# Constant products in front of the transposes and the value products of a fused attention and MoE kernel

## The chip, the cores and the metric

One NeuronCore of one Trainium2 chip. The metric is device time in microseconds, the median of several runs of one launch.

## The reference

Attention with 4 batches, 8 heads, head size 64, 512 local tokens with a window of 32 to either side, and 32 global tokens that attend to all and are attended to by all; then a dense feed-forward layer (512 to 2048 to 512), then a layer of 8 experts that picks one for each of 2176 tokens.

```
s_ll = where(|i - j| <= 32, q_l k_l^T / 8, -1e9);  s_lg = q_l k_g^T / 8
out_l = softmax([s_lg, s_ll]) [v_g, v_l];  out_g = softmax(q_g [k_g, k_l]^T / 8) [v_g, v_l]
x = [out_g, out_l], heads side by side
h = x w_in;  x = max(0.01 h, h) w_out
e = argmax(norm(x) norm(emb)^T / tau);  y = p_e * (relu(x w1[e]) w2[e])
```

## The kernel before

Heads go in twos: 16 head pairs `n`, and each has two score pairs `p` of two 128-row chunks. For one `p`, `S` (L186) adds the mask as a product of `identb` and `mask` into a PSUM bank and the scores on top of it, VectorE takes the maximum (`nm`), ScalarE the exponentials (`pr`), VectorE divides. `TR` (L235) transposes the probabilities of one unit (`p` has two units `u`) into the bank `pp`, four transposes, and ScalarE copies them to `pT`. `AV` (L244) multiplies them with the values into the bank `av`, 16 products, and ScalarE or VectorE copies the result to `xr`. `QK` (L157) transposes queries and keys; `GS`, `GT` and `GA` do the same for the global tokens of two head pairs (`sg`, `gp`, `ga`).

`att_parts` (L975) lays these parts into 68 slots, one unit each: `S` in the even slots, `TR` two units and `AV` four units behind. Slots 0 to 20 run alone (`while slot < SLOT0`). In that time the banks come from the table `ALONE`; `pp` has the two buffers of tag `Y` for itself, `av` shares tag `T`. From slot 21 on the remaining slots are dealt out among the steps of the feed-forward layer (`L1` gives `hps` and `gf`, `L2` gives `yp`), and `bank` is another table.

The feed-forward weights come as 8-byte numbers and are converted on the chip, 32 pieces: `conv_load` fetches `raw` (512 KB, two buffers), `conv_round` makes `t` from it (ScalarE, two instructions), `conv_bits` joins the halves (VectorE, three instructions), `conv_split` casts to the high part (ScalarE) and subtracts for the low part (GpSimd). `conv()` stands in most slots of the alone part and in each of the first feed-forward steps, and the pieces must be done before the steps that use them.

TensorE runs in the order in which the code is written (`manual_schedule`). At this place of the program the other engines and the SP queue are ordered by a scheduler, by priorities and a timeline of its own.

Of the kernel before, what the change touches and what calls it, by code (L numbers as in the profile page):

```python
# [24 lines left out]
def kernel(  # L25
# [16 lines left out]
    nc = tc.nc  # L42
# [5 lines left out]
    E, _, F2 = w1.shape  # L48
# [6 lines left out]
    WK = WIN + SG  # L55
# [48 lines left out]
    def load_v(n):  # L104
# [21 lines left out]
    mask = att.tile([P, 3, WK], BF16, name="mask")  # L126
    nc.vector.memset(mask, 0.0)
    nc.gpsimd.affine_select(
        out=mask[:, :, 0:WIN], in_=mask[:, :, 0:WIN], pattern=[[0, 3], [1, WIN]],
# [3 lines left out]
        out=mask[:, :, 0:WIN], in_=mask[:, :, 0:WIN], pattern=[[0, 3], [-1, WIN]],  # L133
# [6 lines left out]
    identb = att.tile([P, P], BF16, name="identb")  # L140
# [8 lines left out]
    ALONE = dict(sp0="S", sp1="H", sg1="S", pp="Y", av="T", gp="Y", gq="T", ga="T", qp="T", kp="H", gnp="S")  # L149
    bank = ALONE  # L150

    def bank_of(name):
        return bank[name] if name in bank else "T"
# [32 lines left out]
    def S(p):  # L186
# [45 lines left out]
        for h in range(2):  # L232
            units[2 * p + h] = pr2[h]

    def TR(u):  # L235
        pr = units[u]
        pp = ps.tile([P, 4, P], F32, tag=bank_of("pp"), name="pp")
        for j in range(4):
            nc.tensor.transpose(pp[:, j, :], pr[:, j // 2, (j % 2) * P:(j % 2) * P + P], ident)  # L239
        pT = att.tile([P, 4, P], F32, tag="PT", bufs=2, name="pT")  # L240
        nc.scalar.copy(pT, pp)
        units[u] = pT

    def AV(p):  # L244
        n, c0 = p // 2, 2 * (p % 2)
        b, hp = n // HP, n % HP
        pTs = [units.pop(2 * p + h) for h in range(2)]
        ve, vb = values[n]
        av = ps.tile([P, 2, P], F32, tag=bank_of("av"), name="av")
        for i in range(2):  # L250
            for j, v in enumerate((ve, vb)):
                for h in range(2):
                    nc.tensor.matmul(  # L253
                        av[D * h:D * h + D, i, :], v[:, c0 + i, h, :], pTs[h][:, 2 * i + j, :],
                        start=(j == 0), stop=(j == 1), tile_position=(0, D * h),
                    )
        k = 2 * b + p % 2
        if hp == 0:
            xraw[k] = sb.tile([P, KM, 256], F32, tag="xr", bufs=4, name="xr")
        if hp == HP - 1:  # L260
            rows_done.add(k)
        (nc.vector.tensor_copy if p % 2 else nc.scalar.copy)(xraw[k][:, hp, :].rearrange("k (c s) -> k c s", c=2), av)
# [712 lines left out]
    def att_parts(n):  # L975

        parts = []
        m = n // 4
        if m % 2 == 1 and n % 4 == 0 and m < NHP:
            parts.append(lambda: GS(m))  # L980
        if n < NU and n % 2 == 0:
            parts.append(lambda: ahead(50, S, n // 2))
        if 1 == 1 and n % 4 == 3 and m + 1 < NHP:
            parts.append(lambda: ahead(50, QK, m + 1, 1))
        if (n - AVL) % 2 == 0 and 0 <= n - AVL < NU:
            parts.append(lambda: ahead(0, AV, (n - AVL) // 2))
        if m % 2 == 1 and n % 4 == 3 and m < NHP:
            parts.append(lambda: GA(m))
        if 0 <= n - LAG < NU:
            parts.append(lambda: ahead(50, TR, n - LAG))  # L990
        if m % 2 == 1 and n % 4 == 2 and m < NHP:
            parts.append(lambda: GT(m))
        for v in range(2, NHP):
            if n == 4 * (v - 2) + max(AVL + 2, 7 - v % 2):
                parts.append(lambda v=v: load_v(v))
        if n in (AVL + 12, AVL + 14):
            parts.append(lambda: split_x((n - AVL - 12) // 2))
        if n % 4 == 1 and m + 1 < NHP:
            parts.append(lambda: ahead(50, QK, m + 1, 0))
        if 1 == 0 and n % 4 == 3 and m + 1 < NHP:  # L1000
            parts.append(lambda: ahead(50, QK, m + 1, 1))
        return parts
# [57 lines left out]
    while k < len(steps):  # L1060
# [18 lines left out]
        bank = FUSED if (i, f) < (2, 1) else MIXED  # L1079
# [11 lines left out]
        n = (len(halves) + 1) // 2  # L1091
# [136 lines left out]
```

## Time and profile before

| | |
|---|---|
| time, median of 3 runs | 917.76 us (916.94 to 918.02) |
| profiled execution | 921.5 us, span 919.7 us |
| mean granted TensorE clock | 0.965 of full |
| TensorE busy | 869.8 us (95%), 5600 products |
| VectorE, ScalarE, GpSimd busy | 623.5, 566.3, 191.1 us |
| moved by DMA | 92.67 MB |

Busy time is the time in which an engine had an instruction under way. The ends of TensorE's products are modelled, so neighbours overlap in their lengths, and the distance between starts is the better price of one. A granted clock of 1.00 is 2.4 GHz, of 0.50 it is 1.2 GHz.

### The profile page before, as it was taken

The numbers are of one execution on the slowest core, as the hardware profiler recorded it, in microseconds if no ns is written. First come the engines' busy times: TensorE is split into PE (matmuls) and PEld (weight loads), VectorE is DVE, ScalarE is ACT, GpSimd is POOL, SyncE is SP. The second block draws the span as 40 slices with busy tenths as digits, with TensorE's granted clock in tenths as the row PEclk, the third lists the DMA queues.
The fourth block names the chain that finished last, engine by engine and source line by source line (L and its number), as shares of the span: only waits on it lengthen the run. The fifth ranks groups of instructions, "written<-read, shape, count | busy, mean of one in ns | idle before, by whom it ended". The sixth has DMA issues, their size and how long they took to land.

```text
span 919.7 us, 15811 instructions
## 1 busy us (share of the span) xinstructions
PE 869.8 (95%) x5600; PEld 726.0 (79%) x5600; DVE 623.5 (68%) x1419; ACT 566.3 (62%) x1243; POOL 191.1 (21%) x220
## 2 busy tenths in 40 slices
PE   6778789999999999999999999997999999999997
PEld 3546577888888888888888889886787888888885
DVE  6788788444563645463543425557998999999996
ACT  6887776544544645444533223347887888888885
POOL 3433434000200110010000000020366322231211
PEclk7787799999999999999999999999999999999999
DMA  8786463120122021110000000560316119729550
GB/s 233 188 207 176 127 169 93 27 53 12 32 63 45 20 58 34 33 36 9 1 24 1 24 1 22 190 225 12 47 36 229 58 46 338 282 85 383 184 203 26
DMA packets 104994, 92.67 MB, mean 101 GB/s; under 512 B 73735, under 2 KB 82055, under 8 KB 104914
## 3 DMA queue, kind: packets, MB, share of 16 engines
q1 hardware_dynamic: 98290, 78.52, 27.7%
q0 software_dynamic: 4224, 10.78, 4.1%
q10 hardware_dynamic: 2400, 2.36, 0.9%
q8 instruction: 45, 0.74, 0.4%
q14 instruction: 35, 0.29, 0.1%
HBM read 140.03 MB, written 11.63 MB: 165 GB/s over the span
## 4 chain that ended last, share of the span: by engine, by line
PE 72%; DMA 8%; issue 6%; DVE 5%; ACT 5%; POOL 2%; SPq 0%; POOLq 0%; ACTq 0%; DVEq 0%
PE hps L680 21%; PE hp L910 8%; PE yp L702 7%; PE yp L938 7%; PE yp L704 7%; PE yp L703 6%; PE av L253 3%; PE pp L239 3%; PE sp L202 2%; DMA out_dram<-yo,ids 2%; POOL xg L854 2%; DMA ids<-idl 1%; ACT pr L223 1%; PE ga L314 1%; PE lp L504 1%
## 5 line engine op out<-in xcount | busy, mean ns | idle before, releaser
L687 ACT COPY gf<-hps 128x256 f32<-128x256 f32 (+1 forms) x144 | 50.2, 360 | 179.4 <-PE hps L680 178.6
L688 DVE SCALAR_TENSOR_TENSOR gf<-gf 128x256 f32<-128x256 f32 (+1 forms) x144 | 59.7, 422 | 137.2 <-ACT gf L687 136.7
L910 PE MATMUL hp<-w1s,xgT 128*128 128x512 f32 x528 | 137.7, 409 | 3.1 <-DVE xgT L899 3.1
L938 PE MATMUL yp<-w2s,ht 128*128 128x512 f32 x528 | 131.0, 396 | 1.0 <-DVEq L1192 1.0
L938 PEld LDWEIGHTS yp<-w2s,ht 128*128 128x128 f32 x528 | 98.8, 188 | 25.6 <-DVEq L1192 1.4
L910 PEld LDWEIGHTS hp<-w1s,xgT 128*128 128x128 f32 x528 | 98.1, 193 | 24.9 <-DVE xgT L899 4.4
L702 PE MATMUL yp<-woh,g 128*128 128x512 f32 x272 | 115.2, 424 | 0.2 <-ACT g L690 0.2
L704 PE MATMUL yp<-woh,g 128*128 128x512 f32 x272 | 108.0, 397 | 1.1 <-DVE g L691 1.1
L703 PE MATMUL yp<-wol,g 128*128 128x512 f32 x272 | 107.9, 397 | 0.0
L691 DVE TENSOR_TENSOR g<-gf,g 128x256 fp32r<-128x256 f32 (+1 forms) x144 | 60.7, 431 | 42.9 <-ACT g L690 39.9
L680 PE MATMUL hps<-xs,wih 128*128 128x256 f32 x448 | 75.8, 291 | 2.7 <-ACT gf L687 2.7
L690 ACT CAST g<-gf 128x256 fp32r<-128x256 f32 (+1 forms) x144 | 55.4, 395 | 34.2 <-DVE gf L688 34.0
L680 PEld LDWEIGHTS hps<-xs,wih 128*128 128x128 f32 x448 | 65.1, 190 | 9.2 <-ACT gf L687 3.1
L680 PE MATMUL hps<-xs,wil 128*128 128x256 f32 x448 | 71.7, 282 | 0.0
L680 PE MATMUL hps<-xl,wih 128*128 128x256 f32 x448 | 71.7, 282 | 0.0
L946 POOL DMA_INDIRECT out_dram<-yo,ids x22 | 33.8, 1537 | 143.6 <-ACT yo L945 129.7
L704 PEld LDWEIGHTS yp<-woh,g 128*128 128x128 f32 x272 | 51.4, 189 | 14.5 <-DVE g L691 2.1
L680 PEld LDWEIGHTS hps<-xs,wil 128*128 128x128 f32 x448 | 61.4, 190 | 0.0
L680 PEld LDWEIGHTS hps<-xl,wih 128*128 128x128 f32 x448 | 61.4, 190 | 0.0
L702 PEld LDWEIGHTS yp<-woh,g 128*128 128x128 f32 x272 | 51.5, 189 | 12.0 <-issue 4.3
L854 POOL DMA_INDIRECT xg<-x2d,ids x24 | 48.2, 2010 | 60.9 <-PE hps L680 21.6
L865 DVE TENSOR_TENSOR w2s<-w2a,w2s 128x1024 fp32r<-128x1024 f32 x48 | 56.4, 1216 | 3.1 <-ACT w2s L864 3.1
(261 smaller groups left out, 1751.5 us busy)
## 6 DMA issues: line engine op xcount, KB each, us to landing
w1a<-in_moe_w_dram SPq DMA_DIRECT2D x12, 2048.0 KB
w2a<-in_moe_w_dram SPq DMA_DIRECT2D x12, 2048.0 KB
w1b<-in_moe_w_dram SPq DMA_DIRECT2D x12, 2048.0 KB
w2b<-in_moe_w_dram SPq DMA_DIRECT2D x12, 2048.0 KB
raw<-in_moe_w_in_dram SPq DMA_DIRECT2D x14, 512.0 KB
raw<-in_moe_w_out_dram SPq DMA_DIRECT2D x14, 512.0 KB
x2d<-x SPq DMA_DIRECT2D x16, 256.5 KB
kn<-in_k_l_dram SPq DMA_DIRECT2D x31, 128.0 KB
```

The costliest lines, as they stand in the source:

```text
L680: nc.tensor.matmul(hps, ws[a][:, k], xs[c][k], start=(a + c + k == 0), stop=((a, c) == (1, 0) and k == KM - 1))
L687: nc.scalar.copy(gf, hps[:, cs])
L688: nc.vector.scalar_tensor_tensor(out=gf, in0=gf, scalar=0.01, in1=gf, op0=ALU.mult, op1=ALU.max)
L690: nc.scalar.copy(g[:, 0], gf)
L691: nc.vector.tensor_tensor(out=g[:, 1], in0=gf, in1=g[:, 0].bitcast(F32), op=ALU.subtract)
L702: nc.tensor.matmul(yp, g[:, 0], hi, start=(f == 0), stop=False)
L703: nc.tensor.matmul(yp, g[:, 0], lo, start=False, stop=False)
L704: nc.tensor.matmul(yp, g[:, 1], hi, start=False, stop=(f == KF - 1))
L854: nc.gpsimd.indirect_dma_start(out=xg, out_offset=None, in_=x2d[:, :], in_offset=bass.IndirectOffsetOnAxis(ap=ids[:, s:s + 1].bitcast(U32) ...
L865: nc.vector.tensor_tensor(out=w[:, 1, c], in0=src[:, c], in1=w[:, 0, c].bitcast(F32), op=ALU.subtract)
L910: nc.tensor.matmul(hp_, xT[:, a, k, :], w[:, c, k, :], start=(a + c + k == 0), stop=(c == 1 and k == KM - 1))
L938: nc.tensor.matmul(yp, ht[:, a, f, :], w[:, c, f, :], start=(j + a + c + f == 0), stop=(j == c == 1 and f == 3))
```

## The change

While `bank` is `ALONE` (slots 0 to 20), `TR` and `AV` first issue products of `identb` and `mask` into the bank that they have just been given, with start and stop set, so that the products proper overwrite them: 5 ahead of the transposes of an even unit, 2 ahead of those of an odd one (448 columns each), and 8 ahead of the value products (256 columns each).

```diff
+    def spin(out, n):
+
+        if bank is not ALONE:
+            return
+        o = out.rearrange("p a b -> p (a b)")
+        m = min(o.shape[1], 2 * WK)
+        for _ in range(n):
+            nc.tensor.matmul(
+                o[:, 0:m], identb, mask.rearrange("p a b -> p (a b)")[:, 0:m], start=True, stop=True
+            )
+
     def TR(u):
         pr = units[u]
         pp = ps.tile([P, 4, P], F32, tag=bank_of("pp"), name="pp")
+        spin(pp, 5 if u % 2 == 0 else 2)
         for j in range(4):
...
         av = ps.tile([P, 2, P], F32, tag=bank_of("av"), name="av")
+        spin(av, 8)
         for i in range(2):
```

TensorE, the transposes of the two units of the second score pair, and the keys of the next head pair behind them, before:

```order
L253 MATMUL av<-pT,vb_104 64x128 x2
L239 MATMUL pp<-ident,pr_98 128x128 x8
L174 MATMUL kp<-ident,kn 128x128 x4
L179 MATMUL gnp<-ident,gn 128x64
L197 LDWEIGHTS identb
```

And with the change, from the first of the two units on:

```order
L251 MATMUL pp<-ident,pr_98 128x128 x4
L242 LDWEIGHTS identb
L242 MATMUL pp<-mask,identb 128x448
L242 LDWEIGHTS identb
L242 MATMUL pp<-mask,identb 128x448
L251 MATMUL pp<-ident,pr_98 128x128 x4
L174 MATMUL kp<-ident,kn 128x128 x4
```

The eight transposes that stood together have two products between them; five more stand ahead of the first four, and eight of 256 columns ahead of the value products. Over the program there are 68 and 72 of them. The order of TensorE's other instructions is unchanged.

VectorE, from the division of the eighth score pair to the maximum of the ninth (`t` is a weight conversion, three rows each; `nm` the maximum), before:

```order
L229 TENSOR_TENSOR pr_98<-pr_98,sm 128x4x224
L370 SCALAR_TENSOR_TENSOR t_1164<-t_1163,t_1164 128x512
L373 TENSOR_SCALAR t_1163<-t_1163 128x512
L318 COPY xgl<-ga 128x2x32
L374 ISA t_1163<-t_1163,t_1164 128x1024
L370 SCALAR_TENSOR_TENSOR t_1201<-t_1200,t_1201 128x512
L212 TENSOR_REDUCE nm<-sp 128x2 x2
```

And with the change:

```order
L229 TENSOR_TENSOR pr_98<-pr_98,sm 128x4x224
L383 SCALAR_TENSOR_TENSOR t_1341<-t_1340,t_1341 128x512
L386 TENSOR_SCALAR t_1340<-t_1340 128x512
L387 ISA t_1340<-t_1340,t_1341 128x1024
L383 SCALAR_TENSOR_TENSOR t_1395<-t_1394,t_1395 128x512
L331 COPY xgl<-ga 128x2x32
L386 TENSOR_SCALAR t_1394<-t_1394 128x512
L387 ISA t_1394<-t_1394,t_1395 128x1024
L383 SCALAR_TENSOR_TENSOR t_1461<-t_1460,t_1461 128x512
L386 TENSOR_SCALAR t_1460<-t_1460 128x512
L387 ISA t_1460<-t_1460,t_1461 128x1024
L212 TENSOR_REDUCE nm<-sp 128x2 x2
```

Three conversions stand where one and the start of a second stood, and a fourth follows between this maximum and the division.

VectorE at the last of the 32 conversions (`gf` is a feed-forward step), before:

```order
L370 SCALAR_TENSOR_TENSOR t_2113<-t_2112,t_2113 128x512
L227 TENSOR_SCALAR sm<-sm 128x4
L373 TENSOR_SCALAR t_2112<-t_2112 128x512
L228 RECIPROCAL sm<-sm 128x4
L374 ISA t_2112<-t_2112,t_2113 128x1024
L688 SCALAR_TENSOR_TENSOR gf<-gf 128x256
```

And with the change:

```order
L383 SCALAR_TENSOR_TENSOR t_2253<-t_2252,t_2253 128x512
L704 TENSOR_TENSOR g<-gf,g 128x256
L386 TENSOR_SCALAR t_2252<-t_2252 128x512
L701 SCALAR_TENSOR_TENSOR gf<-gf 128x256
L387 ISA t_2252<-t_2252,t_2253 128x1024
L217 ISA pr_97,nm<-sp,mask 128x224
```

The `gf` behind the last conversion is the tenth of VectorE before; with the change the `gf` ahead of its last row is the sixth. On ScalarE, 20 conversions were finished ahead of the first `gf`, and 24 are now.

## Rows read from the trace of the kernel before

**Rows 1.** The page's 40 slices of the span: the granted TensorE clock in tenths.

```profile
PEclk7787799999999999999999999999999999999999
```

**Rows 2.** Busy time by program stage: us, then engines with instructions, clock, DMA share, GB/s.

```profile
12.70:97.00 84.30, 66.97 (x506) 45.68 (x505) 69.03 (x137) 68.45 (x191) 33.43 (x38) 0.76 0.73 192
97.00:112.00 15.00, 8.82 (x38) 7.28 (x38) 13.00 (x24) 11.80 (x33) 6.54 (x6) 0.66 0.52 149
112.00:157.00 45.00, 40.81 (x315) 34.16 (x314) 39.81 (x86) 34.26 (x85) 19.16 (x15) 0.96 0.49 134
157.00:300.00 143.00, 142.99 (x1123) 123.33 (x1122) 70.17 (x260) 68.71 (x209) 11.65 (x23) 1.00 0.16 37
```

The five busy columns are TensorE's products, its weight loads, VectorE, ScalarE and GpSimd.

**Rows 3.** The same view, stretches at the lower clock; the last lies in 112 to 157 us.

```profile
12.70:22.90 10.20, 8.06 (x40) 4.38 (x38) 8.68 (x17) 8.66 (x26) 4.36 (x5) 0.50 0.88 229
...
29.70:36.60 6.90, 5.84 (x31) 4.18 (x31) 5.77 (x15) 5.65 (x15) 4.14 (x8) 0.51 0.85 224
...
40.00:46.80 6.80, 6.80 (x54) 5.01 (x52) 2.88 (x6) 3.95 (x8) 2.56 (x2) 0.50 0.76 225
...
57.10:60.50 3.40, 3.16 (x18) 1.26 (x20) 3.40 (x10) 3.40 (x12) 0.12 (x1) 0.51 0.66 148
...
67.30:74.10 6.80, 6.28 (x34) 4.46 (x33) 6.09 (x11) 5.12 (x16) 1.33 (x2) 0.50 0.58 177
...
77.50:84.40 6.90, 6.90 (x63) 5.25 (x61) 5.65 (x8) 3.79 (x9) 2.73 (x2) 0.51 0.64 168
...
139.00:142.40 3.40, 3.40 (x16) 2.95 (x16) 3.17 (x6) 3.14 (x7) 1.64 (x1) 0.50 0.20 55
```

**Rows 4.** TensorE's waits, 12 to 97 us: us in total, times, longest.

```profile
PE sp L197 <- ACT pr L223: 6.9, 4, 2.7
PE ga L314 <- ACT gt L299: 3.1, 2, 1.6
PE sg L274 <- DVE xr L262: 2.2, 1, 2.2
PE av L253 <- ACT pT L241: 2.1, 4, 0.8
PE pp L239 <- DVE pr L229: 2.0, 2, 1.4
PE qp L162 <- DVE xr L262: 1.6, 2, 0.9
```

**Rows 5.** TensorE's timeline at 67 us: start, us, instruction, idle before it.

```profile
67.82 0.53 PE L197 MATMUL sp<-mask,identb 128*128 128x448 bf16 x1 [2.74 <-ACT pr L223]
```

**Rows 6.** The chain that ended last, 77 to 86 us: start, us, what.

```profile
77.21 2.54 PE ga L314 x40
...
80.80 0.75 PE sp L197 x2
...
84.87 1.02 PE pp L239 x8
```

**Rows 7.** TensorE's timeline, products of 256 columns at the two clock levels.

```profile
106.48 1.05 PE L680 MATMUL hps<-xl,wih 128*128 128x256 f32 x4
107.33 1.06 PE L680 MATMUL hps<-xs,wil 128*128 128x256 f32 x4
...
127.14 0.63 PE L680 MATMUL hps<-xl,wih 128*128 128x256 f32 x4
127.61 0.63 PE L680 MATMUL hps<-xs,wil 128*128 128x256 f32 x4
```

**Rows 8.** Groups of VectorE's instructions, 12.7 to 97 us: busy, mean ns, idle before.

```profile
L370 DVE SCALAR_TENSOR_TENSOR t<-t,t 128x512 int32<-128x512 int32 x17 | 13.6, 805 | 5.6 <-ACT t L363 4.1 <-ACT t L364 1.6
L374 DVE CUSTOM_DVE_ANT_0 t<-t,t 128x1024 uint16<-128x1024 uint16 x17 | 11.5, 684 | 0.1
...
L373 DVE TENSOR_SCALAR t<-t 128x512 int32<-128x512 int32 x17 | 9.5, 570 | 0.6
```

**Rows 9.** TensorE's waits, 97 to 160 us.

```profile
PE pp L239 <- ACT gf L687: 2.8, 1, 2.8
```

## The prediction

> **What bounds the kernel now.** I read the page in slices first, for the clock; then the table of busy times over stretches that I cut by program stage and by clock; then TensorE's waits and the chain of waits; last the rows that give a price.
>
> The slices show TensorE's granted clock at full for the whole run but for the first eighth [rows 1]. The stage table says what that eighth is [rows 2]. From 12.7 to 97 us the attention runs alone: TensorE is busy 66.97 of 84.3 us at a mean clock of 0.76, VectorE 69.03 and ScalarE 68.45, so three engines are near 80% and none is full. From 97 to 112 and from 112 to 157 us the first feed-forward steps run, while the conversion of their weights still goes on; there TensorE is busy 8.82 of 15 and 40.81 of 45 us. From 157 us it is busy 142.99 of 143 us. So whatever brings TensorE earlier to its place of 157 us moves the end by as much, and nothing behind it changes.
>
> The stretches at the lower of the two clock levels (1.2 GHz, shown as 0.50 or 0.51) lie in rows 3. Six are in the alone stage, 41.0 us long, with 8.06 + 5.84 + 6.80 + 3.16 + 6.28 + 6.90 = 37.0 us of busy TensorE; at 2.4 GHz half of that, 18.5 us, would not be there. TensorE's 84.3 us are therefore 48.5 us of work at full clock, 18.5 us lost to the clock and 17.3 us idle. The clock falls when TensorE has waited. The longest wait, 2.7 us of a mask product for the exponentials of the tile before, ends at 67.82 us, and the clock is down from 67.3 us [rows 3 to 5]; `ga` begins at 77.21 us behind a copy of ScalarE, one of its two waits (3.1 us in all), and the clock is down from 77.5 us [rows 3, 4, 6].
>
> **The change, part by part.**
>
> *The products.* `TR` now issues 5 or 2 products of 448 columns ahead of its transposes, `AV` 8 of 256 columns ahead of its own, in slots 0 to 20 only. That is 10 x 5 + 9 x 2 = 68 and 9 x 8 = 72. Four products of 256 columns start in 127.14 to 127.61 us at full clock and in 106.48 to 107.33 us at the lower [rows 7]: 0.118 and 0.213 us each. By columns 448 is 0.206 and 0.372 us (estimate); the chain has two of just that shape at the lower clock in 0.75 us [rows 6], which agrees. Sum: 68 x 0.206 + 72 x 0.118 = 22.5 us of TensorE at full clock, 40.6 us if all of it ran at the lower. Nothing reads these products, and they need no new DMA.
>
> *What covers them.* They are free where TensorE waits at those two places. That is 2.0 us for `pp` and 2.1 us for `av`; 13.8 us of waits are at the mask products, `ga`, `sg` and `qp`, where nothing is added [rows 4]. A later arrival there does eat into these waits, since most are for work that started earlier on ScalarE or VectorE; but `ga` waits for a copy of what TensorE itself made just before, and that wait comes along. So the direct cover is 4.1 us, the cover by arrival up to another 10.7 us (13.8 less 3.1).
>
> *What the clock gives back.* Between 0 and 18.5 us. I expect the falls behind the mask products and the group scores to go (those gaps shrink by about the 2 us of products that a pair now has ahead of them) and the two falls behind `ga` to stay. Their stretches have 6.80 + 6.90 us busy, so 6.9 us stay lost; the products inside them, about 17 in each, cost 2.8 us more each at the lower clock. TensorE's need is then 48.5 + 6.9 + 22.5 + 5.6 = 83.5 us, against the 84.3 us that the stage has. It just fits: the clock pays for the products, and TensorE gains next to nothing in this stage. Since 8.7 us of the chain in one stretch are TensorE's, from `ga` at 77.21 us to the end of the transposes at 85.89 us [rows 6], a gain or loss of a few us there would show. Ends for this term: -6 (all at 2.4 GHz, need 71.0 us, other engines then set the pace) and +14 us (below).
>
> The Trainium skill, "TensorE: Matmul & The Clock Gate", Part 1 (what's actually happening), says to model the warm-up penalty as under 1% of a typical span. That would be 9.2 us here, and it would cap what this change can win from the clock at 9 us. The 18.5 us above are 2% of the span, so by the rows the rule does not hold for this kernel, and I leave the end at 18.5.
>
> *What the order moves.* TensorE's order is the written one; ScalarE, VectorE, GpSimd and SP are ordered by the scheduler, which now sees a longer TensorE and puts weight conversions into the room. Counted in the two orders, 24 of 32 conversions on ScalarE precede the first feed-forward step (20 before), and the last one comes on VectorE right behind the sixth step instead of ahead of the tenth. Each costs VectorE 805 + 570 + 684 ns [rows 8], 2.06 us with the overlap of neighbours counted twice; I take 1.6 to 2.06, so 6.5 to 8.2 us more in the alone stage, where VectorE has 84.3 - 69.0 = 15.3 us idle. ScalarE pays about the same. VectorE would be at 90 to 92%; it fits, with little to spare, and four conversions in a row stand ahead of one score tile's reduction, which the raw loads must feed. I take +1.5 us (ends 0 and +8).
>
> What it gives back lies behind the stage. In 112 to 157 us TensorE loses 4.2 us idle and half of the 3.40 us at the lower clock, 1.7 us, together 5.9 us; the largest wait there is one of 2.8 us, on a ScalarE copy [rows 2, 3, 9]. With the conversions over three steps earlier nothing of that kind is left to wait for: -5.9 us (ends -6 and 0). The loss in 97 to 112 us, 6.2 us idle and 3.7 us of clock, I leave: the steps there still carry three to four conversions per pair and VectorE is busy 13.00 of 15 us.
>
> *Sum.* 0 + 1.5 - 5.9 = -4.4 us. The profiled execution took 921.5 us, so 917.1 us beside it; it lies 3.7 us above the median, and against the median of 917.76 us I forecast 913.4 us. A measurement of this kernel can tell about 0.2%, 1.8 us, from no change.
>
> **The rivals.**
>
> *Slower: the products fill TensorE.* The place is the alone stage, the price is the clock. If the falls keep coming because most waits are not where the products are, the products run half at the lower clock (about 31.5 us) and TensorE needs 48.5 + 18.5 + 31.5 = 98.5 us of 84.3: +14, less the 5.9, +8 us. With four of the six stretches left it is 92.3 us, +8 and in all +2. It decides from a need of about 90 us on. For it: only 4.1 us of the waits are at the two places. Against it: the added columns stand close to the gaps, and clock and gaps feed each other. About +5 us, 922.8 us.
>
> *Much faster: the clock stays up.* Need 71.0 us, TensorE is no longer the pace of the stage, which then goes with VectorE's 77.2 us at about 95%, 81 us: -3; then -5.9, and the 3.7 us of clock in 97 to 112 us: 905 us. Against it: the `ga` waits, and VectorE nearly full.
>
> *Nothing: VectorE and ScalarE set the pace.* Then the four conversions lengthen the alone stage by 6 to 7 us and give back 5.9 later: 917.8 us.
>
> **How the numbers follow.** Forecast 0.46 (its own range 909 to 916.5), slower 0.28, much faster 0.12, nothing 0.14. Faster by over 0.2% is 0.46 + 0.12 = 0.58; same 0.14; slower 0.28. The likeliest time is 913.4 us. The range goes from 905 us, which leaves out half of the much faster case, to 923 us, which leaves out the upper half of the slower one: 0.06 + 0.14, 0.20 left out.
>
> **What would show it.** Right: the mean clock of the alone stage at 0.85 to 0.92, two stretches at the lower level left and both behind `ga`; the first feed-forward product at 96 to 100 us; no wait over 1 us on TensorE from 30 us behind it on. Wrong: a clock still near 0.76 and a first feed-forward product past 104 us (slower); VectorE above 93% in the stage with the end unmoved (nothing); ScalarE waiting for raw loads in the run of four conversions, which I priced at almost nothing.

## The result, and the profile after

The changed kernel takes 923.69 us (median of 5 runs, 922.31 to 925.68), the kernel before 917.76 us in the same comparison (916.2 to 918.57): ratio 1.0062, interval 1.0044 to 1.0079. The change costs 5.9 us. The forecast was 913.4 us, faster.

The slices first. The clock of the first eighth, which the change aims at, did rise (compare [rows 1]):

```profile
PEclk9889999999999999999999999999999999999999
```

The profile after, busy time by stretch (us, then TensorE's products, its weight loads, VectorE, ScalarE, GpSimd, the granted clock, the DMA share). The second boundary is the first feed-forward product, the last the fourth round of group scores, which stood at 96.50 and 159.10 us before:

```profile
12.70:60.00 47.30, 40.44 (x306) 26.64 (x305) 39.53 (x74) 38.03 (x104) 20.30 (x23) 0.93 0.83 213
60.00:109.70 49.70, 41.01 (x337) 26.80 (x337) 47.39 (x85) 42.35 (x114) 20.89 (x20) 0.90 0.69 188
109.70:130.70 21.00, 16.00 (x117) 12.82 (x115) 20.65 (x42) 17.65 (x45) 10.12 (x9) 1.00 0.51 147
130.70:163.00 32.30, 32.30 (x255) 28.51 (x255) 20.52 (x50) 18.23 (x49) 6.06 (x6) 0.95 0.27 67
```

Against [rows 2] the stage in which the attention runs alone (to the first feed-forward product) is 13.2 us longer although its clock went from 0.76 to 0.91. VectorE is busy 47.39 of 49.7 us in its second half (95%; 90% over the stage), where 82% was the mean before. Behind the stage 9.2 of the 13.2 us come back: from the first feed-forward product to the fourth group scores it is 53.4 us, before 62.6 us. TensorE ends that stretch without a gap, 32.30 of 32.30 us. So the fourth group scores are 3.9 us late:

```profile
163.03 1.08 PE L286 MATMUL sg<-kT,gz 64*32 64x512 f32 x8
```

From there on the two traces run in parallel. The first expert product (`hp`) is 461.5 us behind this point before and 461.6 us behind it after, and from there to the end it is 299.1 and 297.3 us. So between the two traces the change costs 2.3 us, all of it placed; the rest of the 5.9 us is that the profiled execution of before was 3.7 us above its median, and where it lost them no trace shows. The last part varies by itself: in the traces of all kernels whose loads are whole it takes 295.0 to 300.8 us, with the same code.

The clock did most of what was asked of it. Of the six low stretches of the alone stage, 41.0 us [rows 3], four are left, some 17 us: a long one behind `ga`, and three of about 3.5 us, one again behind `ga` and two behind waits for `qz` and `xr`. First the windows, then TensorE's timeline ahead of each:

```profile
41.00:47.50 6.50, 6.50 (x45) 4.40 (x44) 6.01 (x9) 3.76 (x8) 3.36 (x2) 0.50 0.78 188
...
64.90:68.40 3.50, 3.50 (x26) 2.18 (x26) 3.50 (x9) 2.27 (x8) 1.28 (x1) 0.55 0.92 254
...
81.50:85.00 3.50, 3.50 (x34) 2.65 (x32) 3.33 (x7) 2.04 (x4) 1.75 (x2) 0.53 0.88 231
...
102.20:105.60 3.40, 3.40 (x23) 1.08 (x22) 3.05 (x7) 2.25 (x5) 0.97 (x2) 0.50 0.54 122
```

```profile
40.31 0.72 PE L327 MATMUL ga<-gt,ve 128*64 128x32 f32 x16 [1.23 <-ACT gt L312]
...
64.16 1.42 PE L202 MATMUL sp<-kT,qz 64*128 64x224 f32 x8 [1.95 <-ACT qz L164]
...
80.85 0.66 PE L327 MATMUL ga<-gt,ve 128*64 128x32 f32 x16 [1.84 <-ACT gt L312]
...
100.96 0.66 PE L162 MATMUL qp<-ident,qn 128*128 128x128 f32 x4 [1.94 <-DVE xr L275]
```

TensorE's waits of the changed kernel from 12 to 110 us (total, times, longest). The mask products' wait of [rows 4] is down from 6.9 to 2.5 us, and waits for `qz` (new) and for `xr` ahead of `qp` (1.6 before) are the largest:

```profile
PE sp L202 <- ACT qz L164: 4.0, 2, 2.1
PE qp L162 <- DVE xr L275: 3.9, 3, 1.9
PE ga L327 <- ACT gt L312: 3.1, 2, 1.8
PE sp L197 <- ACT pr L223: 2.5, 3, 1.2
PE av L266 <- ACT pT L253: 1.9, 3, 0.9
```

The chain of work that ended last, 60 to 131 us, is nearly half the weight conversion on VectorE (`t`), 47.5%; in the same stretch of before the three lines have 4.4, 4.4 and 3.8%:

```profile
by line: DVE t L383 20.3%; DVE t L386 14.9%; DVE t L387 12.3%; issue 8.7%; DVE pr L229 7.6%; DVE nm L212 5.5%; ACT pr L223 4.3%; DVE sm L227 3.2%; PE sg L286 2.7%; POOL wil L395 2.2%; DVE gf L701 2.0%; DVE pr L217 1.7%; DVE xl L673 1.5%; DV
```

The groups of that conversion, 12.7 to 110 us, answer to [rows 8]: 22 or 23 instead of 17 of each kind, and 919 + 832 + 553 ns, 2.30 us for one conversion where it was 2.06. Together they take 52.0 us of VectorE, before 34.6.

```profile
L383 DVE SCALAR_TENSOR_TENSOR t<-t,t 128x512 int32<-128x512 int32 x22 | 20.2, 919 | 3.6 <-ACT t L376 2.6 <-ACT t L377 1.1
L387 DVE CUSTOM_DVE_ANT_0 t<-t,t 128x1024 uint16<-128x1024 uint16 x23 | 19.1, 832 | 0.3
...
L386 DVE TENSOR_SCALAR t<-t 128x512 int32<-128x512 int32 x23 | 12.7, 553 | 0.5
```

So two things could have cost the time, the products and the order that the scheduler made around them. The experiments take them apart. Each ratio stands against runs of the kernel before that were taken beside it. Points in the table at the end of the experiments come from one trace each.

### The profile page after: what moved, and what is told of

It reads as the page before. It is cut to its first block, busy times and chain, and to the rows that moved or that the text cites. A ratio compares the mean times of both kernels' runs of the same rounds, so it can differ in the third digit from the quotient of the medians.

```text
span 922.0 us, 16077 instructions
## 1 busy us (share of the span) xinstructions
PE 879.9 (95%) x5740; PEld 730.6 (79%) x5740; DVE 628.5 (68%) x1419; ACT 567.0 (62%) x1243; POOL 191.1 (21%) x220
## 4 chain that ended last, share of the span: by engine, by line
PE 68%; DVE 10%; DMA 8%; issue 7%; ACT 3%; POOL 3%; SPq 0%; POOLq 0%; ACTq 0%; DVEq 0%
PE hps L693 21%; PE yp L715 7%; PE hp L923 7%; PE yp L716 7%; PE yp L717 7%; PE yp L951 6%; PE av L266 2%; POOL xg L867 2%; PE pp L251 2%; PE sp L202 2%; DMA out_dram<-yo,ids 2%; DVE t L383 2%; DMA raw<-in_moe_w_in_dram 2%; DMA ids<-idl 1%; DVE t L386 1%
## 5 line engine op out<-in xcount | busy, mean ns | idle before, releaser
L701 DVE SCALAR_TENSOR_TENSOR gf<-gf 128x256 f32<-128x256 f32 (+1 forms) x144 | 57.7, 409 | 141.0 <-ACT gf L700 140.6
L704 DVE TENSOR_TENSOR g<-gf,g 128x256 fp32r<-128x256 f32 (+1 forms) x144 | 58.3, 413 | 43.3 <-ACT g L703 36.8
L959 POOL DMA_INDIRECT out_dram<-yo,ids x22 | 34.6, 1574 | 141.4 <-ACT yo L958 128.8
```

What stands on the lines that cost most here:

```text
L701: nc.vector.scalar_tensor_tensor(out=gf, in0=gf, scalar=0.01, in1=gf, op0=ALU.mult, op1=ALU.max)
L704: nc.vector.tensor_tensor(out=g[:, 1], in0=gf, in1=g[:, 0].bitcast(F32), op=ALU.subtract)
```

## The experiments

### Products and order, each alone

The order of ScalarE, VectorE, GpSimd and SP was written down from both kernels, and edges that wait for nothing fix one or the other, from the start into the feed-forward steps. TensorE keeps its written order.

```diff
+            for eng, ranks in ORDER.items():
+                seq = traced[eng]
+                for a, b in zip(ranks, ranks[1:]):
+                    tc.add_manual_dep(
+                        seq[b], seq[a].name,
+                        mybir.DependencyInfo(mybir.DependencyClass.NoSync, mybir.DependencyReason.DATA), reason="order",
+                    )
```

The changed kernel with the order of before:

> The added products stay, but ScalarE, VectorE, GpSimd and SP are held to the order that they had before the change (edges between neighbours on one engine, no waits). Order theory (the 6 us are lost because the scheduler moved weight conversions into the part where attention runs alone, where VectorE is then full): the loss goes, 912 to 918 us, first feed-forward product back at 90 to 98 us, clock of the alone stage near 0.9. Product theory (the 22 us of added products delay TensorE): the loss stays, 922 to 926 us, first feed-forward product past 102 us.

Measured: 924.21 us, ratio 1.0048 (1.0033 to 1.0064).

The kernel before, without products, with the order of the changed one:

> No added products, but ScalarE, VectorE, GpSimd and SP are held to the order that they have with the change. Order theory: the loss is there without a single added product, 921 to 930 us, first feed-forward product at 106 us or later, clock of the alone stage near 0.75, and if the products do pay for themselves it is slower than the change (923.7 us). Product theory: no loss, 914 to 919 us.

Measured: 926.41 us, ratio 1.0083 (1.0062 to 1.0104).

And, run later, the kernel before with its own order fixed:

> The kernel before with ScalarE, VectorE, GpSimd and SP fixed to their own old order by the same edges as in the runs before: a control. If the edges cost nothing: ratio 1.000 (917 to 920 us), first feed-forward product at 94 to 99 us, fourth group-score product at 156 to 160 us. If fixing the order costs by itself: above 1.003, and then part of the +4.4 us of the products in the old order is not theirs.

Measured: 919.51 us, ratio 1.0005 (0.9992 to 1.0018), so the edges cost nothing that can be told. This run is the control from here on. Its trace is of the longest of its ten executions, 924 us, and has both points later than expected: the first feed-forward product at 100.22 us where before's had it at 96.50. Two executions of one order differ by 3.7 us there, and a difference of that size between single traces proves nothing.

By the times, then, the products alone cost 1.0048 less 1.0005, 0.43% or 4.0 us (by the intervals 2 to 6). The order alone costs 0.78%, 7.2 us (5 to 9), as much as the whole change or more. In the new order the products cost nothing that can be told: 1.0062 with them, 1.0083 without, and the intervals overlap. With the products the new order costs nothing that can be told either: 1.0062 with it, 1.0048 without. So each alone is enough to lose the time, taking out one of them does not bring it back, and the two costs do not add.

The windows from 12.7 us to the first feed-forward product show what each does to the stage. In turn the products in the old order, the order without products, and the control:

```profile
12.70:102.80 90.10, 77.10 (x642) 52.10 (x641) 70.68 (x140) 70.34 (x197) 32.46 (x38) 0.91 0.71 184
```

```profile
12.70:108.00 95.30, 70.58 (x502) 48.01 (x502) 84.81 (x153) 77.86 (x210) 40.06 (x42) 0.80 0.74 197
```

```profile
12.70:100.20 87.50, 63.25 (x502) 44.47 (x502) 69.44 (x135) 68.71 (x191) 33.12 (x38) 0.84 0.72 185
```

Busy and idle time of TensorE: 77.1 and 13.0 us with the products, 70.6 and 24.7 us with the order alone, 63.3 and 24.2 us in the control; 67.0 and 17.3 us in [rows 2]. So the idle time of one order differs by 6.9 us between its two traces. The changed kernel has 81.4 of 97 us, 15.6 idle. The control is also a warning on the clock: against [rows 2] it has 0.84 instead of 0.76 and 3.7 us less busy time, and it comes to its first feed-forward product later.

TensorE's waits at the places of the change and around them, 12 to 100 us in the control and 12 to 103 us with the products in the same order:

```profile
PE sp L203 <- ACT pr L229: 8.7, 6, 2.7
PE pp L245 <- DVE pr L235: 4.2, 2, 2.8
PE sg L280 <- DVE xr L268: 2.8, 1, 2.8
PE av L259 <- ACT pT L247: 2.5, 3, 1.4
PE ga L320 <- ACT gt L305: 1.5, 1, 1.5
PE ga L320 <- DVE t L379: 1.3, 1, 1.3
```

```profile
PE sp L203 <- ACT pr L229: 4.9, 4, 2.4
PE ga L333 <- ACT gt L318: 3.7, 2, 2.2
PE av L272 <- ACT pT L259: 1.3, 2, 0.6
PE sg L293 <- DVE xr L281: 1.0, 1, 1.0
PE pp L257 <- DVE pr L235: 0.8, 1, 0.8
```

The waits shrink at the two places and also where no product was added (mask products, `sg`); of the larger ones only those of `ga` grow. The waits for `qz` and `xr` of the changed kernel come with the order, which has them without any product, 12 to 108 us:

```profile
PE qp L168 <- DVE xr L268: 4.9, 3, 3.0
...
PE sp L208 <- ACT qz L170: 3.0, 2, 2.0
```

### What makes the order dear

Theory: VectorE is full, and four more conversions there push the stage out. If so, a conversion that costs VectorE little takes the difference away.

```diff
+        full, t, low = t, t[:, 0:1, 0:P], low[:, 0:1, 0:P]
         nc.vector.scalar_tensor_tensor(
...
-        temps[i] = t
+        temps[i] = full
```

> No products, old order; VectorE's three instructions of a weight conversion work on 128 of 512 columns, so the converted weights are wrong. It is the base for the next run. Both theories: the alone stage is shorter than before (17 conversions at about 2 us of VectorE each lose over half), 895 to 912 us.

> The same small VectorE part, in the new order, no products. If the new order costs because VectorE is full of conversions, most of its 7.6 us go: 0 to 3 us over the run with the old order. If it costs because ScalarE stands in its fixed order waiting for raw loads or because the other engines wait for one another in a worse sequence, 5 to 9 us over it remain.

Measured: 913.12 us (0.9946, 0.9926 to 0.9965) in the old order, 1 us above its forecast, 919.19 us (1.0007, 0.9987 to 1.0027) in the new one. The difference between the orders stays, 0.61%, 5.6 us. VectorE's load is worth 5 us by itself, but easing it alone does not remove that difference. (The wrong weights do not show behind the stage: the last part takes 296.1 and 295.0 us.) ScalarE's waits from 20 to 95 us say what took its place, first in the old order, then in the new one:

```profile
ACT t L370 <- DMA raw<-in_moe_w_in_dram: 2.2, 1, 2.2
ACT t L370 <- DMA raw<-in_moe_w_out_dram: 1.1, 1, 1.1
```

```profile
ACT t L370 <- DMA raw<-in_moe_w_in_dram: 9.1, 4, 3.9
ACT t L370 <- DMA raw<-in_moe_w_out_dram: 4.2, 3, 1.8
```

With the VectorE step short, 13.3 us of waits for raw weights stand there, 3.3 us in the old order. So the loads were tried next: from the third conversion on only one of 128 partitions is loaded, into two tiles that stay.

```diff
+            part = slice(0, P if i < 2 else 1)
-            (nc.scalar if 2 <= i < 6 else nc.sync).dma_start(t, src.bitcast(I32))
+            (nc.scalar if 2 <= i < 6 else nc.sync).dma_start(t[part], src.bitcast(I32)[part])
```

> No products, old order; raw loads from the third on bring 1 of 128 partitions, so the weights are wrong, and loads are no longer waited for. Base for the next run: 900 to 915 us.

> The same small raw loads, in the new order, no products. If the new order costs because ScalarE waits for raw loads behind which the softmax stands, its 7.6 us go: 0 to 3 us over the run with the old order. If VectorE being full is the cause, 5 to 9 us over it remain.

Measured: 931.19 us (1.0142, 1.0118 to 1.0167) and 939.03 us (1.0222, 1.0189 to 1.0256). The forecast of 900 to 915 us is missed, for a reason behind the stage: from the first expert product to the end the runs take 313.7 and 313.8 us, before it was 299.1. In that part of the old-order run TensorE waits 19.0 us for ScalarE's `hs`, before 5.1, with the same number of products; why stays open. Between the two orders 0.8%, 7.3 us, stay. With the loads gone VectorE is the full one, 42.23 of 44 us from 60 to 104 us in the new order:

```profile
60.00:104.00 44.00, 31.13 (x249) 23.16 (x248) 42.23 (x74) 36.78 (x94) 19.20 (x19) 0.81 0.25 56
```

Neither is the cause by itself. With VectorE eased, waits for the loads take its place; with the loads eased, VectorE is full. No run eases both together, so it is not shown that these two make up the difference, and a worse sequence among the engines, a rival in the expectation, stays possible. A second theory remains: what matters is how many conversions stand ahead of the first feed-forward step at all, whichever engine pays.

### Which products cost

`AV`'s 72 products alone, `TR`'s 68 alone, in the old order:

```diff
-        spin(pp, 5 if u % 2 == 0 else 2)
```

> Old order, only the 72 products of 256 columns ahead of the value products (8.5 us of TensorE at full clock, estimate). Product theory (each us of product that TensorE does not wait out goes to the end, less what the clock gives back): about a third of the 4.4 us of all products in the old order, 0 to +3 us over the kernel before. If only the clock matters: at or under the kernel before.

```diff
-        spin(av, 8)
```

> Old order, only the 68 products of 448 columns ahead of the transposes (14 us at full clock, estimate). Product theory: +2 to +5 us over the kernel before, more than with the value products alone. If only the clock matters: at or under the kernel before.

Measured: 919.31 us (1.0005, 0.9986 to 1.0024) and 921.8 us (1.0033, 1.002 to 1.0047). `AV`'s are free within the measurement, `TR`'s cost 0.28% over the control, 2.6 us (by the intervals 1 to 4).

Then 22 products at the places where TensorE was seen to wait and the clock to fall, ahead of `ga` and of the second round of group scores (against the changed kernel; `ga` also gets a tile of a whole bank):

```diff
-        spin(pp, 5 if u % 2 == 0 else 2)
...
-        spin(av, 8)
...
+        if n == 3:
+            spin(sg1.rearrange("p (a b) -> p a b", a=4), 8)
...
-        ga = ps.tile([P, 2, SG], F32, tag=bank_of("ga"), name="ga")
+        ga = ps.tile([P, 4, P], F32, tag=bank_of("ga"), name="ga")
+        spin(ga, 7)
+        ga = ga.rearrange("p a b -> p (a b)")[:, 0:2 * SG].rearrange("p (m s) -> p m s", m=2)
```

> Old order, no products at the two places of the change; instead 7 of 448 columns ahead of each group value product and 8 ahead of the second group score in the alone stage (22 products, 4.5 us at full clock), which stand where TensorE waited and the clock fell. Product theory: the products lie under waits, the falls behind them go, 912 to 918 us, that is -5 to 0 us against the kernel before, clock 0.975 or more. If clock and waits of TensorE do not decide this stage: within 1.5 us of the kernel before although the clock rises.

Measured: 925.46 us (1.0074, 1.0052 to 1.0096), a miss by 7 us at the least, for products worth 22 x 0.206 = 4.5 us at full clock. The clock did not rise: over the program the five longer executions have 0.967 to 0.974, the kernel before 0.966 to 0.979 in the same comparison. The profiled execution was the fastest of the six, 920.05 us, so its trace does not show what makes the others longer, and whether the larger tile has a part in it was not tried. That is open.

### Conversions held back

The second theory can be tried from the other side. A feed-forward step needs only its own two conversions, and from 157 us on VectorE and ScalarE are busy 70.17 and 68.71 of 143 us [rows 2]. Here conversions are issued less often in the alone stage, and an edge keeps the first ScalarE step of each behind the attention or feed-forward instruction that is written just ahead of it:

```diff
-        if slot % 2 < 1 or slot in (1, 3, 5):
+        if slot % 2 < 1:
             conv()
...
+            if behind is not None:
+                tc.add_manual_dep(
+                    last_of("Activation", 1), behind.name,
+                    mybir.DependencyInfo(mybir.DependencyClass.NoSync, mybir.DependencyReason.DATA), reason="late",
+                )
```

> The kernel before, no products, with the conversions held back: 11 on ScalarE ahead of the first feed-forward copy instead of 20, the last one ahead of the 21st instead of the 12th. Theory (the number of conversions ahead of the first feed-forward step sets when TensorE's full stretch begins, and that stretch has VectorE and ScalarE half idle from 157 us on): first feed-forward product at 86 to 93 us, fourth group-score product at 146 to 153 us, time 908 to 913 us. Rival (attention's own chain and the clock set the alone stage): first product within 2 us of 96.5 us, time 916 to 920 us. Second rival (held-back conversions come late for the steps that read them): TensorE waits for woh or wih behind 120 us, time above 920 us.

Measured: 908.78 us, ratio 0.9883 (0.9858 to 0.9908). First feed-forward product at 87.98 us, fourth group scores at 144.92 us. Time and first product lie where the theory put them, the group scores 1 us ahead of it, and neither rival's numbers came. The scheduler was free to order the other instructions here, so the run shows what holding back gains with the order that comes of it.

The same edit with the products of the change:

> The same with the products of the change. With the conversions out of the way TensorE's clock and its waits are more of what sets the alone stage. If the products pay there: below the late conversions alone by 1 to 4 us, clock of the alone stage above 0.90. If their 22.5 us of TensorE cost what they cost in the old order: above it by 2 to 5 us.

Measured: 917.18 us, ratio 0.998 (0.9965 to 0.9996), 8.4 us above the run without them, more than either forecast. The order is fixed in neither of the two. By their traces the number of conversions ahead of each of VectorE's first eleven divisions is the same to within one, but other instructions changed places, so how much of the 8.4 us is order was not taken apart. The windows from 12.7 us to the first feed-forward product, without and with them:

```profile
12.70:88.00 75.30, 58.84 (x503) 41.87 (x502) 51.67 (x117) 56.40 (x172) 22.14 (x30) 0.86 0.64 156
```

```profile
12.70:99.40 86.70, 76.46 (x642) 52.14 (x641) 53.28 (x120) 59.22 (x178) 20.05 (x30) 0.92 0.57 142
```

TensorE gets 17.6 us more to do, clock gain included, and its idle time falls from 16.5 to 10.2 us. The stage grows by the rest, 11.4 us. VectorE is at 61% there, so it is not full. TensorE's waits from 12 to 88 us again shrink at the mask products, from 5.0 to 0.7 us, and grow at `ga`, from 1.6 to 5.6 us; 3.5 of these end with a conversion step on ScalarE.

With `slot % 3 < 1`, 8 conversions ahead, no products:

> No products, 8 conversions ahead of the first feed-forward copy, the last ahead of the 22nd. Theory: first feed-forward product another 1 to 4 us earlier than with 11, the time 0 to 3 us below it, unless attention's chain already sets the stage, then the same within 2 us. If steps have to wait for their weights, TensorE shows waits behind 110 us and the time is longer.

Measured: 906.5 us, ratio 0.9869 (0.9852 to 0.9885). This is the best version: 12.0 us below the kernel before, and by the medians 1.9% below the changed one. First feed-forward product at 84.57 us, fourth group scores at 142.56 us. Some of it is given back: from those scores to the first expert product it is 465.1 us, before 461.5; conversions now share that stretch.

| kernel | first feed-forward product, us | fourth group scores, us | time against before |
|---|---|---|---|
| before | 96.50 | 159.10 | 1 |
| before, order fixed | 100.22 | 161.59 | 1.0005 |
| products, old order | 102.78 | 161.42 | 1.0048 |
| new order, no products | 108.01 | 163.46 | 1.0083 |
| the change | 109.71 | 163.03 | 1.0062 |
| short VectorE step, old / new order | 94.39 / 106.43 | 152.84 / 160.74 | 0.9946 / 1.0007 |
| `AV`'s only / `TR`'s only, old order | 99.04 / 100.94 | 159.25 / 160.96 | 1.0005 / 1.0033 |
| at group places, old order | 99.12 | 159.44 | 1.0074 |
| small loads, old / new order | 96.71 / 103.98 | 156.25 / 161.65 | (longer last stage) |
| 11 conversions ahead | 87.98 | 144.92 | 0.9883 |
| the same with products | 99.38 | 154.45 | 0.998 |
| 8 conversions ahead | 84.57 | 142.56 | 0.9869 |

In each pair the new order puts the first feed-forward product 7 to 12 us later and the fourth group scores 2 to 8 us later. What comes back between the two points is time that TensorE had idle or at the lower clock there: in the changed kernel its idle time goes from 10.4 to 5.0 us, its busy time from 52.2 to 48.3. Its busy time is 48.3 to 52.7 us in all these traces, and the stretch is never under 53 us.

## Why the prediction was wrong

*"From 157 us TensorE is full, so whatever brings it earlier to its place moves the end as much."* Right, in every trace that leaves the conversions where they were.

*"What the order moves", +1.5 us.* Wrong, and the largest miss: with what it gives back the order was to gain 4.4 us, and alone it costs 7.2 us by the times. It put the first feed-forward product 11.5 us later (7.8 us against the control's trace). The step that failed is the price of the four conversions, "6.5 to 8.2 us more in the alone stage", held against 15.3 us of idle time: "it fits, with little to spare". With the order alone VectorE is busy 15.4 us longer there (84.81 us, the control 69.44), and in the changed kernel its conversions alone take 17.4 us more (52.0 us, before 34.6). The four conversions were rightly counted in the order, but 22 or 23 run ahead of the first feed-forward product where 17 ran, and one takes 2.30 us, above the upper end of 2.06. That is all the idle time that there was, and not all of it can be used: 10.5 us stay idle with the order alone. The share of VectorE, 90%, came out as forecast, because the stage grew with the work. VectorE is not the whole of it: with its step short the order still costs 5.6 us. Then ScalarE waits 13.3 us for raw loads, which I priced "at almost nothing"; in the changed kernel itself these waits are 6.5 us in the stage, before 2.3. My own "nothing" rival had this mechanism, with 6 to 7 us on the alone stage and 5.9 back.

*"Gives back", -5.9 us.* The mechanism was right. The stretch to the fourth group scores shrank by 9.2 us in the changed kernel and by 7.1 us with the order alone, 5.9 us if the control's trace is the base. Against the trace of before, part of the idle time and of the low clock of 97 to 112 us, which I left out, came back too. But all this only refunds what the same move had cost earlier. The conversions have to be done anyway; ahead of the first feed-forward step they delay TensorE's long list of work.

*The products, 0 us.* The sum of busy time was good: 83.5 us forecast, 81.4 measured in the changed kernel and 77.1 in the old order. The step that failed is "against the 84.3 us that the stage has. It just fits". From 67.0 to 83.5 us TensorE would have had to use 16.5 us of its 17.3 us of idle time, more than my own two covers together, 4.1 and at most 10.7 us. In the old order 4.3 us of idle time were used against the trace of before and 11.2 us against the control's, and 13.0 us stayed; 6.3 us were used with the conversions held back, and 10.2 stayed. So the products cost 4.0 us in the old order. Both covers are real: in the pair of one order the waits at the two places shrink by 4.6 us (`pp` 3.4, `av` 1.2) and those at the mask products and `sg` by 5.6 us. How large they are, single traces cannot say, since the idle time of one order alone differs by 6.9 us. That the waits of `ga` come along was right, and they grow: from 2.8 to 3.7 us there, from 1.6 to 5.6 us with the conversions held back.

*The clock.* Foreseen: 0.85 to 0.92, and two stretches left, both behind `ga`. Measured 0.93 and 0.90 in the two halves, and four stretches, two of them behind `ga` and two behind waits for `qz` and `xr`, which the new order has without the products too. The clock gave back less than the products need: with the conversions held back it rises from 0.86 to 0.92, and busy time still grows by 17.6 us. The Trainium skill, "TensorE: Matmul & The Clock Gate", Part 1, says to model the warm-up penalty as under 1% of a span. That sentence speaks of the ramp at a kernel's start, and the falls of [rows 3] come again behind waits, so the 9 us that I drew from it is no bound on what they cost. By TensorE's busy time the clock gave back 4 to 8 us in the changed kernel (an estimate: 22.5 us of products by [rows 7], and 81.4 us busy where the control has 63.3 and [rows 2] 67.0), and no run gained time by it that stands clear of the noise.

*The rivals.* "The products fill TensorE" gave 922.8 us, close to the result, and that products cost is real: 4.0 us in the old order. Of its two signs a clock still near 0.76 did not show, a first feed-forward product past 104 us did (109.71). But the new order alone gives both the late product (108.01) and the lost time. That the number came so close is luck: behind it stand products that lengthen the stage by some 11 us (5 and the 5.9 given back), and no cost of the order. The products seem to lie in part in waits that the order made: TensorE's idle time is 15.6 us with them and 24.7 us without. The sign of "nothing" came half, VectorE over 93% in the second half of the stage only, and the end moved.

What stays open: why 22 products at the group places cost as much as 140 elsewhere, and what part of the order's cost is VectorE, the loads or the sequence of the other engines.

## What to carry to other kernels

Work that fills an engine's gaps has to be set against the waits that it can use, not against all idle time of the stage: here 16.5 of 17.3 us were counted on, and 4 to 11 us were used. Where the engine itself feeds what it waits for, as at `ga`, the wait came along and grew, and a better clock can be bought above its worth. After an edit on one engine compare the scheduler's order on the others as well, since that side effect can cost as much as the edit, and fix the order to measure the two apart; free idle time of an engine is no sign that moved work fits. Work done ahead of need is not free when the engine that will be full later is waiting behind it: here holding back conversions gained 12 us, twice what the change lost.

## What the runs showed of the hardware

One conversion step on VectorE (L383) takes 0.67 to 1.76 us in the changed kernel, 0.69 in the median of 23. The slow one below lies beside a subtraction on GpSimd. VectorE from 72 us and GpSimd beside it in the changed kernel (start, us):

```profile
72.28 1.76 DVE L383 SCALAR_TENSOR_TENSOR t<-t,t 128x512 int32<-128x512 int32 x1
```

```profile
71.60 1.90 POOL L395 TENSOR_TENSOR wol<-t,woh 128x512 fp32r<-128x512 f32 x1 [0.59 <-ACT woh L394]
```

GpSimd's runs to 73.50 us, and VectorE's ends 0.54 us later, about the length of a quick one. The Trainium skill, "SBUF — State Buffer", section "SBUF: two separate sides", says that the two share a pair of ports, among others for a VectorE instruction with two inputs in SBUF beside a GpSimd one that reads SBUF, and that the later one blocks until the other is done; these rows agree. The other way round, the subtraction that starts at 80.39 us, while a division and then a conversion step run on VectorE (79.95 to 81.62 us), takes 2.37 us where 1.27 is the usual length. With more conversions in the stage one took 2.30 us where it took 2.06; how much of that is this, no run separates.

The clock alone does not tell how fast a stage goes. Two executions of one order had 0.76 and 0.84 in the alone stage, and the one with 0.84 came out of it 3.7 us later.
